# Linear attention and a residual MLP on one core: a rewrite with two woven TensorE streams

## The chip, the cores and the metric

The kernel runs on one core of a Trainium2 chip. A core has five engines that run side by side and are ordered by semaphores: TensorE (PE), VectorE (DVE), ScalarE (ACT), GpSimd (POOL) and SyncE (SP), which issues most DMAs. The metric is the time of one execution on the device, in microseconds, as the median of several runs. Lower is better.

## The reference

There are 8 batches, 8 heads, 576 tokens and 64 channels a head (512 channels in all). All inputs and the output are float32.

```python
kv  = einsum('bhsd,bhse->bhde', k, v)          # 64 x 64 a head
att = einsum('bhsd,bhde->bhse', q, kv)
att = att / sqrt(mean(att*att, -1) + 1e-6) * g_norm
x   = att as [batch, token, 512]
a1  = alpha1 * x + beta1
u   = x + lam * einsum('ts,bsd->btd', w_tok, a1)    # w_tok 576 x 576
a2  = alpha2 * u + beta2
out = u + lam * (relu(a2 @ w_ch1) @ w_ch2)          # 512 -> 2048 -> 512
```

## The kernel before, in words

A batch's 576 tokens are 4 chunks of 128 (tokens p*4 + c, so that one partition loads 4 adjacent tokens) and a tail of 64. Weights and the moving side of the MLP are bf16; the attention runs in f32r, a rounded float32 with 4 bytes.

The steps of a batch, with their lines in the profile:

- Loads on SP's queue: `load_main` (L324) and `load_tail` (L330) bring k, v and q as float32 into `kf`, `vf`, `qf` and the tails.
- Rounding on DVE: `round_kv` (L347, L351) and `permute_q` (L355) copy them to f32r and put the 4 chunks outermost.
- `kv_groups` (L366, L369): for each pair of heads five matmuls with 128 tokens (the last 64) in the contraction; the moving side is 256 columns, four heads of v. Only the two diagonal 64 x 64 blocks of the result are used. DVE (L389) copies each times g_norm into `kvc`, and ACT (L392) copies it once more without g, so that `kvc` gives both the scaled and the plain result.
- `qt_groups` (L407, exits L414 and L420): 20 PE transposes of q.
- `qkv_groups` (L451): for each of 5 chunks four matmuls of 256 columns, one a pair of heads: 128 columns with g and 128 without. ACT squares the plain half (L459), DVE sums (L461), ACT takes the root (L464), DVE inverts (L467), multiplies (L471, this is x), forms `rt` = x * alpha1 * lam (L476) and adds beta1's share (L480).
- `tok_groups` (L496): for each of 5 chunks five matmuls of 512 columns with the transposed w_tok; the odd tail chunk computes 128 rows of which 64 are used. DVE adds (L502). POOL forms a2 = u * alpha2 + beta2 in two passes (L506, L509).
- `ut_groups` (L527, exit ACT L533): PE transposes of a2 in bf16, the tails of two batches together.
- `ch1_groups`: an even batch has 16 x 4 matmuls of 512 columns (L560), an odd one 16 x 8 of 320 columns (L575), which take in the tails of both batches. ACT applies relu into `ht` (L551).
- `ch2_groups` (L597): 16 matmuls of 512 columns for each of 4 chunks (5 in odd batches). DVE adds u (L606); SP stores (L609, L613). lam is in `w2` already: it was multiplied in when w_ch2 was loaded (DVE and POOL, L746); w_ch1 is cast by ACT (L736).

The order of the work is a planner's. Every operation is recorded with an engine, a cost in us, what it reads and writes, and a priority (its place in the program). `schedule` plays the engines forward with these costs: each takes the first operation in its queue that is ready, PE from the first 8, the others from the first 400, and PSUM banks are given out in pairs or singly. The resulting order on each engine is then fixed and only semaphores act on the chip. A PE operation is a whole group (4 to 16 matmuls), so groups of different steps alternate but matmuls within a group are together:

```python
for b in range(NB):
    ch1, ch2 = list(ch1_groups(b)), list(ch2_groups(b))
    ...
    merge(ch1, list(qkv_groups(b + 1)), 0, len(ch1) * 5 // 8)
    ...
    for f in tok_groups(b + 1):
        f()
    merge(ch2[:8], [], 0, 0)
    ...
    merge(ch2[8:], fill, 0, len(ch2) - 10)   # fill: ut(b+1), kv(b+2), qt(b+2)
```

At the start q, k, v of batch 0, w_tok and six vectors (each broadcast to 128 partitions by its DMA) are loaded first, then the weights. w_tok is transposed by PE in float32 (L674, exits ACT L679) and its row sums are formed by DVE (`wsums`, L691).

Of the kernel before, what the change touches and what calls it, by code (L numbers as in the profile page):

```python
# [13 lines left out]
NB = 8  # L14
# [5 lines left out]
TP = 640  # L20


class Op:
    __slots__ = ("eng", "cost", "fn", "deps", "raw", "alloc", "tiles", "pri", "idx",
                 "start", "end", "pos", "waits", "inc", "lat", "clock", "sem")

    def __init__(self, eng, cost, fn, pri, idx):
        self.eng, self.cost, self.fn, self.pri, self.idx = eng, cost, fn, pri, idx
        self.deps, self.raw = set(), set()
        self.alloc, self.tiles = [], []  # L30
        self.start = self.end = self.pos = None
        self.waits, self.inc, self.lat, self.clock, self.sem = [], False, 0.0, None, None


class PTile:


    def __init__(self, prog, n):
        self.prog, self.n, self.bank, self.ops, self.prev = prog, n, None, [], set()

    def ap(self, parts=slice(0, 128)):
        return self.prog.ps[parts, self.bank:self.bank + self.n, :]

    def flat(self, parts=slice(0, 128)):
        return self.ap(parts).rearrange("p b f -> p (b f)")


class Prog:

    COMPUTE = ("PE", "ACT", "DVE", "POOL")

    def __init__(self, nc, stack):
        self.nc, self.stack = nc, stack
        self.ops, self.lastw, self.readers = [], {}, {}
        self.ps = stack.enter_context(nc.psum_tensor("ps", [128, 8, 512], F32))
        self.eng = {"PE": nc.tensor, "ACT": nc.scalar, "DVE": nc.vector,
                    "POOL": nc.gpsimd, "SP": nc.sync, "AQ": nc.scalar}
        self.bias = 0  # L60
        self.pe_window = 8

    def ptile(self, n):
        return PTile(self, n)

    def op(self, eng, cost, fn, r=(), w=(), pri=0.0, dma_us=None):
        o = Op(eng, cost, fn, len(self.ops) + pri + self.bias, len(self.ops))
        o.lat = dma_us
        self.ops.append(o)
        for key in r:  # L70
            if isinstance(key, PTile):

                o.deps.update(y for y in key.ops if y.eng != eng)
                key.ops.append(o)
                o.tiles.append(key)
# [4 lines left out]
        for key in w:  # L80
            if isinstance(key, PTile):
                if not key.ops:
                    o.alloc.append(key)
                key.ops.append(o)
                o.tiles.append(key)
# [8 lines left out]
            self.readers[key] = []  # L94
        return o

    def schedule(self):
        queues = {}
        for o in self.ops:
            queues.setdefault(o.eng, []).append(o)  # L100
        for e, q in queues.items():
            q.sort(key=lambda o: o.pri)
        free = {e: 0.0 for e in queues}
        order = {e: [] for e in queues}
        left = len(self.ops)
        owner = [None] * 8
        dma_free = 0.0
        t = 0.0
        events = set()

        def done(o, t):
            return o.end is not None and o.end <= t + 1e-9

        def bank_ok(b, t):
            tile = owner[b]
            return tile is None or all(done(x, t) for x in tile.ops)

        def bank_since(b):
            tile = owner[b]
            return -1.0 if tile is None else max(x.end for x in tile.ops)  # L120

        def place(tile, t):
            if tile.n == 2:
                c = [b for b in (0, 2, 4, 6) if bank_ok(b, t) and bank_ok(b + 1, t)]
                if not c:
                    return None
                return min(c, key=lambda b: max(bank_since(b), bank_since(b + 1)))
            c = [b for b in range(8) if bank_ok(b, t)]
            if not c:
                return None  # L130
            return min(c, key=lambda b: (bank_ok(b ^ 1, t), bank_since(b)))

        while left:
            progressed = False
            for e, q in queues.items():
                while q and free[e] <= t + 1e-9:
                    pick = None
                    cands = q[:self.pe_window] if e == "PE" else q[:400]
                    for o in cands:
                        if not all(done(y, t) for y in o.deps):  # L140
                            continue
                        if any(place(tile, t) is None for tile in o.alloc):
                            continue
                        pick = o
                        break
                    if pick is None:
                        break
                    q.remove(pick)
                    for tile in pick.alloc:
                        tile.bank = place(tile, t)  # L150
                        for b in range(tile.bank, tile.bank + tile.n):
                            if owner[b] is not None:
                                pick.deps.update(owner[b].ops)
                            owner[b] = tile
                    pick.start = t
                    free[e] = t + pick.cost
                    if pick.lat is not None:
                        dma_free = max(dma_free, t) + pick.lat
                        pick.end = dma_free + 2.0
                    else:  # L160
                        pick.end = t + pick.cost + 0.15
                    pick.pos = len(order[e])
                    order[e].append(pick)
                    events.add(pick.end)
                    events.add(free[e])
                    left -= 1
                    progressed = True
            if left:
                nxt = [x for x in events if x > t + 1e-9]
                if not nxt:  # L170
                    raise RuntimeError("stuck at %r" % t)
                t = min(nxt)
                events = set(nxt)
        self.order = order
        self.sequence = sorted(self.ops, key=lambda o: (o.start, o.idx))

    def queue_of(self, e):
        return "ACT" if e == "AQ" else e

    def synchronize(self):  # L180

        known = {}
        pos = {}
        for o in self.sequence:
            e = self.queue_of(o.eng)
            o.pos = pos.get(e, 0)
            pos[e] = o.pos + 1
            k = known.setdefault(e, {})
            need = {}
            for y in o.deps:  # L190
                ye = self.queue_of(y.eng)
                if y.lat is not None:
                    key, v = ("dma", y.idx), 1
                else:
                    key, v = ye, y.pos + 1
                    if ye == e and e != "POOL" and y not in o.raw:
                        continue
                    if ye == e and e == "PE":
                        continue
# [10 lines left out]
            o.clock = dict(k)  # L210
            if o.lat is not None:
                o.clock[("dma", o.idx)] = 1
                o.inc = True
            else:
                o.clock[e] = o.pos + 1

    def emit(self):
        nc = self.nc
        sems = {e: self.stack.enter_context(nc.semaphore("s_" + e)) for e in self.COMPUTE}
        count = {e: 0 for e in self.COMPUTE}  # L220
        val = {}
        for o in self.sequence:
            if o.lat is not None:
                val[o.idx] = (self.stack.enter_context(nc.semaphore("d%d" % o.idx)), 16)
            elif o.inc:
                count[o.eng] += 1
                val[o.idx] = (sems[o.eng], count[o.eng])
        block = self.stack.enter_context(nc.Block("main"))

        @block.gpsimd  # L230
        def _(gps):
            for o in self.sequence:
                eng = self.eng[o.eng]
                for y in o.waits:
                    eng.wait_ge(*val[y.idx])
                ins = o.fn(eng)
                if o.lat is not None:
                    ins.then_inc(val[o.idx][0], 16)
                elif o.inc:
                    ins.then_inc(sems[o.eng], 1)  # L240
            for o in self.sequence:
                if o.lat is not None:
# [3 lines left out]
def bass_transnormer_attn__then__resmlp_affine_kernel(  # L246
# [15 lines left out]
    with ExitStack() as stack:  # L262
# [5 lines left out]
        ident = sb("ident", [128, 128], F32)  # L268
        identb = sb("identb", [128, 128], BF16)
        e1_bc = sb("e1_bc", [128, DM], F32)  # L270
# [5 lines left out]
        eps = sb("eps", [128, 1], F32)  # L276
        wsum = sb("wsum", [128, 6], F32)
        wsp = sb("wsp", [128, 4], F32)
        kf = sb("kf", [128, NH, 4, DH], F32)
        vf = sb("vf", [128, NH, 4, DH], F32)  # L280
        qf = sb("qf", [128, NH, 4, DH], F32)
# [545 lines left out]
```

## Time and profile before

| | |
|---|---|
| runs | 421.88, 422.67, 422.98 us; median 422.67 |
| span of the profiled execution | 422.0 us, 5398 instructions; the profile gives no time of this execution beside its span |
| median of the runs less the span | 0.65 us |
| busy, share of the span | PE 376.5 us (89%), DVE 226.8 (54%), ACT 167.5 (40%), POOL 120.3 (29%) |
| weight loads on PE (PEld) | 227.8 us (54%) |
| DMA | 49.15 MB, 116 GB/s over the span |
| granted PE clock | 0.964 of full, mean |

How to read it: an engine's busy time is an average over stages. PE is pipelined: the recorded time of a matmul (379 ns for L597) overlaps the next one's, so what a matmul costs is the distance between starts in a run of equal ones. PEld lies beside PE. The chain of waits goes back from the last instruction and names at each step what released it.

### The profile page before, as it was taken

The numbers are of one execution on the slowest core, as the hardware profiler recorded it, in microseconds if no ns is written. First come the engines' busy times: TensorE is split into PE (matmuls) and PEld (weight loads), VectorE is DVE, ScalarE is ACT, GpSimd is POOL, SyncE is SP. The second block draws the span as 40 slices with busy tenths as digits, with TensorE's granted clock in tenths as the row PEclk, the third lists the DMA queues.
The fourth block names the chain that finished last, engine by engine and source line by source line (L and its number), as shares of the span: only waits on it lengthen the run. The fifth ranks groups of instructions, "written<-read, shape, count | busy, mean of one in ns | idle before, by whom it ended". The sixth has DMA issues, their size and how long they took to land.

```text
span 422.0 us, 5398 instructions
## 1 busy us (share of the span) xinstructions
PE 376.5 (89%) x2193; PEld 227.8 (54%) x2193; DVE 226.8 (54%) x371; ACT 167.5 (40%) x263; POOL 120.3 (29%) x92
## 2 busy tenths in 40 slices
PE   0574755899899999999999999999999999999994
PEld 0563242444677465545775565446774665446642
DVE  3439894995587336862786165743783228620011
ACT  1069142540477025712673135503770157215600
POOL 1000499309300830038003800074007400290000
PEclk9985695999999999999999999999999999999999
DMA  8999999202293019501670139001100201011012
GB/s 241 331 349 302 359 265 351 84 0 99 71 282 85 2 75 263 125 1 61 214 163 2 50 124 284 6 26 51 37 2 0 76 25 25 2 50 51 2 50 75
DMA packets 49128, 49.15 MB, mean 116 GB/s; under 512 B 14608, under 2 KB 39184, under 8 KB 49104
## 3 DMA queue, kind: packets, MB, share of 16 engines
q1 hardware_dynamic: 46672, 46.29, 37.7%
q10 hardware_dynamic: 2432, 2.52, 1.9%
q8 instruction: 17, 0.28, 0.3%
q14 instruction: 7, 0.06, 0.0%
HBM read 39.37 MB, written 9.44 MB: 116 GB/s over the span
## 4 chain that ended last, share of the span: by engine, by line
PE 69%; POOL 12%; DVE 7%; DMA 4%; ACT 3%; issue 2%; POOLq 0%; SPq 0%
PE ps L597 22%; PE ps L575 17%; PE ps L560 12%; POOL a1f L506 6%; POOL a2b L509 6%; PE ps L496 6%; PE ps L451 4%; PE ps L407 4%; DMA qf<-in_q_dram 4%; PE ps L366 2%; PE ps L527 1%; DVE xm L480 1%; DVE xm L502 1%; DVE krt L351 1%; PE ps L674 1%
## 5 line engine op out<-in xcount | busy, mean ns | idle before, releaser
L597 PE MATMUL ps<-w,ht 128*128 128x512 bf16 x576 | 135.3, 379 | 0.0
L506 POOL TENSOR_TENSOR a1f<-xm,a_bc 128x512 f32<-128x512 f32 x32 | 42.8, 1337 | 255.3 <-DVE xm L502 253.5
L551 ACT ACTIVATE ht<-ps 128x640 bf16<-128x640 f32 (+1 forms) x96 | 77.8, 810 | 50.2 <-PE ps L560 25.3
L597 PEld LDWEIGHTS ps<-w,ht 128*128 128x128 bf16 x576 | 54.1, 98 | 57.0 <-DVE xm L502 0.6
L575 PE MATMUL ps<-a2t,w 128*128 128x320 bf16 x512 | 73.0, 299 | 0.0
L606 DVE TENSOR_TENSOR xm<-ps,xm 128x512 f32<-128x512 f32 x32 | 22.1, 690 | 83.1 <-PE ps L597 83.0
L533 ACT ACTIVATE a2t<-ps 128x1024 bf16<-128x1024 bf16 (+1 forms) x20 | 18.8, 938 | 116.8 <-PE ps L527 116.8
L560 PE MATMUL ps<-a2t,w 128*128 128x512 bf16 x256 | 61.2, 388 | 2.6 <-ACT a2t L533 1.1
L575 PEld LDWEIGHTS ps<-a2t,w 128*128 128x128 bf16 x512 | 48.7, 98 | 19.9 <-ACT a2t L533 0.3
L509 POOL TENSOR_TENSOR a2b<-a1f,b_bc 128x512 bf16<-128x512 f32 (+1 forms) x40 | 54.2, 1355 | 3.1
L496 PE MATMUL ps<-rt,wt 128*128 128x512 bf16 x200 | 46.9, 393 | 7.5 <-DVE rt L476 7.5
L560 PEld LDWEIGHTS ps<-a2t,w 128*128 128x128 bf16 x256 | 23.8, 100 | 30.4 <-issue 1.8
L366 PE MATMUL ps<-vr,kr 128*128 128x256 f32 x128 | 26.5, 332 | 13.8 <-DVE vrt L351 13.8
L496 PEld LDWEIGHTS ps<-rt,wt 128*128 128x128 bf16 x200 | 20.0, 100 | 32.5 <-DVE rt L476 7.8
L451 PE MATMUL ps<-kvc,qt 128*128 128x256 f32 x160 | 33.2, 338 | 2.7 <-ACT kvc L392 2.7
L461 DVE TENSOR_REDUCE small<-sq 128x8 f32<-128x512 f32 (+1 forms) x40 | 27.1, 677 | 11.4 <-ACT sq L459 11.3
L502 DVE TENSOR_TENSOR xm<-ps,xm 128x512 f32<-128x512 f32 x32 | 22.0, 690 | 16.9 <-PE ps L496 16.7
L366 PEld LDWEIGHTS ps<-vr,kr 128*128 128x128 f32 x128 | 20.3, 206 | 16.9 <-DVE vrt L351 14.3
L451 PEld LDWEIGHTS ps<-kvc,qt 128*128 128x128 f32 x160 | 25.7, 210 | 6.8 <-ACT kvc L392 3.0
L414 ACT ACTIVATE qt<-ps 128x1024 fp32r<-128x1024 f32 x16 | 16.4, 1024 | 22.3 <-PE ps L407 22.3
L480 DVE SCALAR_TENSOR_TENSOR xm<-e_bc,wsum,xm 128x512 f32<-128x512 f32 x32 | 25.0, 782 | 0.2
L459 ACT ACTIVATE sq<-ps 128x512 f32<-128x512 f32 (+1 forms) x40 | 23.6, 591 | 2.9 <-PE ps L451 2.8
(57 smaller groups left out, 294.6 us busy)
## 6 DMA issues: line engine op xcount, KB each, us to landing
kf<-in_k_dram SPq DMA_DIRECT2D x8, 1024.0 KB, 7.4
qf<-in_q_dram SPq DMA_DIRECT2D x8, 1024.0 KB, 9.6
stg<-in_moe_w_ch_dram SPq DMA_DIRECT2D x8, 1024.0 KB, 10.8
out_dram<-xm SPq DMA_DIRECT2D x32, 256.0 KB, 2.3
vf<-in_v_dram SPq DMA_DIRECT2D x7, 1024.0 KB, 9.0
vf<-in_v_dram ACTq DMA_DIRECT2D x1, 1024.0 KB, 9.8
kft<-in_k_dram SPq DMA_DIRECT2D x8, 128.0 KB, 9.3
qft<-in_q_dram SPq DMA_DIRECT2D x8, 128.0 KB, 9.0
```

The lines of the kernel that those rows point to most:

```text
L366: e.matmul(o, flat(kr[:, c, 2 * pr:2 * pr + 2, :]), flat(vr[:, c, u0:u0 + 4, :]), start=(c == 0), stop=False)
L451: m = e.matmul(t.flat()[:, 256 * pr:256 * pr + 256], qt[:, pr, 128 * c:128 * c + 128], kvc[:, pr, :], start=True, stop=True)
L461: P.op("DVE", dve_us(512), lambda e: e.tensor_reduce(out=small[rows, sms], in_=sq[rows, sqs], axis=AX.X, op=ALU.add), r=[("sq", sqs)], w=[ ...
L480: P.op("DVE", dve_us(560), lambda e: e.scalar_tensor_tensor(out=x, in0=e2_bc[rows, :], scalar=wsum[rows, wc:wc + 1], in1=x, op0=ALU.mult, ...
L496: m = e.matmul(t.flat(), wt[:, ws, col:col + 128], rt[:, sc, :], start=(sc == 0), stop=(sc == 4))
L502: P.op("DVE", dve_us(512), lambda e: e.tensor_tensor(out=x, in0=t.flat(rows), in1=x, op=ALU.add), r=[t, xkey(b, c)], w=[xkey(b, c)], pri=-100)
L506: P.op("POOL", pool_us(512), lambda e: e.tensor_tensor(out=a1f[rows, af, :], in0=x, in1=a2_bc[rows, :], op=ALU.mult), r=[xkey(b, c), "a2"] ...
L509: P.op("POOL", pool_us(512), lambda e: e.tensor_tensor(out=a2b[rows, c, :], in0=a1f[rows, af, :], in1=b2_bc[rows, :], op=ALU.add), r=[("a1 ...
L551: P.op("ACT", act_us(n), lambda e: e.activation(dst, src(), ACT.Relu), r=[t], w=key)
L560: m = e.matmul(t.ap()[:, i, :], w1[:, dj, 128 * (fj + i):128 * (fj + i) + 128], a2t[:, dj, 0:512], start=(dj == 0), stop=(dj == 3))
L575: m = e.matmul(t.ap()[:, i, 0:320], w1[:, dj, 128 * fj:128 * fj + 128], a2t[:, dj, 320 * i:320 * i + 320], start=(dj == 0), stop=(dj == 3))
L597: m = e.matmul(t.flat(), ht[:, fj, 128 * c:128 * c + 128], w2[:, fj, :], start=(fj == 0), stop=(fj == 15))
```

## The change

The planner and the body are written anew. What it does:

1. **Two PE streams.** ch1 and ch2 form the stream `main` (PSUM banks 0 to 3), everything else `fill` (banks 4 to 7). `schedule` takes main operations strictly in order and a ready fill operation beside each. A fill operation marked slow (128-column f32) is woven with one main operation: their matmuls alternate one by one. The order on every engine is fixed by the planner as before.
2. **Attention per head over two token chunks.** q, k, v keep the layout of the load. A stationary operand is one head's two adjacent chunks (128 columns: 2 tokens x 64). kv of a head is two matmuls of 128 columns whose two diagonal blocks are added (ACT copies one, DVE adds the other, ACT copies the sum to the lower half), with two more for the tails of 4 heads. q is transposed by matmuls with an f32r identity. att comes from 128-column matmuls, 4 heads to a bank; x and `rm` are formed from it for 2 chunks at once, and g_norm is applied later by POOL (and is folded into alpha1's row for `rm`).
3. **Casting loads.** q from batch 1 on, k and v from batch 2 on, w_tok, w_ch1 and w_ch2 are loaded by DMAs issued on POOL's queue that change the type on the way. DVE's rounding is left for batches 0 and 1 only.
4. **a2 by transposing DMA from the third batch on** (index 2): POOL forms a2 as before, SP issues `dma_start_transpose`. For batches 0 and 1 PE transposes xm and the exit applies alpha2 and beta2.
5. **lam at the PSUM exit.** w2 holds w_ch2 itself; DVE multiplies the exit of ch2 by lam into one of three `tmp` buffers, POOL adds it to u (DVE in the last batch).
6. The tails of two batches are done in one set of tok matmuls with 64-row outputs side by side, ch1 always has 512 columns, with a tail of 128 columns in odd batches. x has four buffers, a2 transposed three. The six vectors are loaded as single rows and broadcast by PE; w_tok's row sums come from one-column matmuls.

The core of the diff, new side (lines as in the new file):

```diff
+    # schedule(), PE's turn
+    m = main[0] if main and can(main[0], t) else None
+    f = None
+    if not (last_fill and m):
+        for o in fill[:10]:
+            if can(o, t, o.margin if m else 0.0):
+                f = o
+                break
+    ...
+    if f is not None and m is not None and f.kind == "w":
+        ...
+        self.sequence.append((f, m))        # woven one by one
```

```diff
-            for src, dst, n in ((kf, kr, "k"), (vf, vr, "v")):
-                P.op("DVE", dve_us(2048, 2), lambda e, s=src, d=dst: e.tensor_copy(
+    def load_kv(b):                                           # L584, L586; q: fill_q L576, L579
+        for n, x, m, tl in (("k", k, kr, krt), ("v", v, vr, vrt)):
+            P.dma("POOL", n + "r", 1 << 20, lambda e, x=x, m=m: e.dma_start(
+                md(m[:]), src_main(x, b, 0, 8)), w=[(n, 0), (n, 1)], issue=1.2)
+            P.dma("POOL", n + "rt", 1 << 17, ...)
+    def load_w1(i):                                           # L520; load_w2 L526; w_tok L512, L515
+        wdma[i] = P.dma("POOL", "w1_%d" % i, 1 << 20, lambda e: e.dma_start(w1[...], moe_w_ch1[...]), ...)
```

```diff
-                        e.matmul(o, flat(kr[:, c, 2 * pr:2 * pr + 2, :]),
-                                 flat(vr[:, c, u0:u0 + 4, :]), ...)                  # 256 columns
+                fns += [lambda e, h=h, o=o, c=c: e.matmul(                         # kv(), L616
+                    t.ap()[:, o], fl(kr[:, h, c:c + 2, :]), fl(vr[:, h, c:c + 2, :]), ...) for c in (0, 2)]
+                    fns.append(lambda e, h=h, c=c, o=o: e.matmul(                  # qtr(), L668; tail L650
+                        t.ap()[:, o], fl(qr[:, h, c:c + 2, :]), identr[:], start=True, stop=True))
+                fns = [lambda e, h=h: e.matmul(                                    # norm(), L701; tail L727
+                    t.ap()[:, 128 * (h % 4):128 * (h % 4) + 128], qt[:, h, cp, :],
+                    kvc[:, i, h, :], start=True, stop=True) for h in range(4 * hh, 4 * hh + 4)]
```

```diff
+        def a2_dma(b, c):                                     # from b = 2; a2_pe L838, L847 before
+            P.op("POOL", ..., a1f[:, s] = x * a2_bc)          # L878
+            P.op("POOL", ..., a2b[:, c] = a1f[:, s] + b2_bc)  # L881
+            P.dma("SP", "t%d" % c, 1 << 18, lambda e: e.dma_start_transpose(dst, a2b[:, c]), ...)  # L885
-                P.op("DVE", dve_us(512), lambda e: e.tensor_tensor(out=x, in0=t.flat(), in1=x, op=ALU.add), ...)
+            P.op("DVE", ..., tmp[:, s] = t.ap() * lam_bc)     # finish(), L944
+            P.op("DVE" if last else "POOL", ..., x = x + tmp[:, s])   # L949
```

Other new lines: ch1 is L900 with its tail L913, ch2 L928, relu L895, tok L800 with the tails L818, bias1 L786, the multiplication by g_norm L778.

## The prediction

> **What bounds the kernel now.** I read the table by stage first: the stages cut at the starts of the channel step (ch1) of each batch.
>
> ```profile
> core 0: us, PE busy (x) PEld busy (x) DVE busy (x) ACT busy (x) POOL busy (x), PEclk, DMA share, GB/s
> ...
> 20.00:45.00 25.00, 13.82 (x65) 11.49 (x63) 17.80 (x39) 16.78 (x26) 0.00 (x0) 0.69 1.09 325
> ...
> 60.00:72.00 12.00, 3.71 (x15) 1.81 (x16) 7.28 (x8) 3.02 (x6) 11.92 (x6) 0.65 1.03 328
> ...
> 163.20:206.46 43.26, 42.55 (x240) 23.83 (x238) 24.66 (x43) 18.18 (x28) 12.69 (x10) 1.00 0.36 99
> 206.46:253.60 47.14, 47.14 (x307) 30.58 (x305) 26.86 (x45) 20.48 (x36) 12.66 (x10) 1.00 0.40 111
> ```
>
> There are two regimes. From 116 us to the end PE is busy in all but 0.7 us of each pair of stages, at full clock; an even and an odd batch together take 43.26 + 47.14 = 90.4 us, and no other engine reaches 60%. Up to 72 us the DMA engines are full (325 GB/s) and PE is half idle at a low clock. The chain of waits in order of time shows how that start ends, and gives clean rates for long runs of one matmul:
>
> ```profile
> 59.40 2.23 POOL a1f L506
> ...
> 64.87 2.25 POOL a2b L509
> 67.17 1.05 PE ps L527 x8
> 68.24 1.03 ACT a2t L533
> 69.32 3.61 PE ps L560 x8
> ...
> 135.94 5.40 PE ps L496 x25
> ...
> 157.60 0.87 PE ps L407 x8
> ...
> 383.10 16.30 PE ps L575 x120
> 399.39 17.28 PE ps L597 x80
> 416.70 0.69 DVE xtl L606
> ```
>
> The first ch1 matmul starts at 69.3 us, behind POOL's two passes for a2, transposes and an eviction. A 512-column bf16 matmul costs 0.216 us (5.40/25, 17.28/80), a 320-column one 0.136, a 128-column f32 transpose 0.109 (0.87/8). After the last matmul 422.0 - 416.7 = 5.3 us remain. The timeline of PE prices the rest:
>
> ```profile
> 119.58 0.74 PE L451 MATMUL ps<-kvc,qt 128*128 128x256 f32 x4
> 120.17 3.43 PE L575 MATMUL ps<-a2t,w 128*128 128x320 bf16 x24
> 123.33 0.75 PE L451 MATMUL ps<-kvc,qt 128*128 128x256 f32 x4
> 123.92 2.35 PE L575 MATMUL ps<-a2t,w 128*128 128x320 bf16 x16
> ```
>
> From 120.17 to 123.92 are 3.75 us; 24 x 0.136 = 3.27 of them are L575, so four 256-column f32r matmuls cost 0.48, or 0.120 each. L366 with L369, taken the same way, costs 0.118 each. Eight 128-column bf16 transposes (L527) between two L597 runs cost 0.056 each.
>
> **Attention at N=128 and weaving.** Before, a pair of batches has main work (ch1 and ch2) of 64 x 0.217 + 128 x 0.136 + 144 x 0.216 = 62.4 us, and 28.0 us of the rest: 50 tok matmuls 10.8, 40 kv 4.7, 40 qkv 4.8, 40 q transposes 4.4, 36 a2 transposes 2.0, idle and switching 1.3. After, main is 256 + 16 matmuls of 512 columns and 64 of 128: 272 x 0.216 + 64 x 0.056 = 62.3, the same. The attention keeps its counts (40 kv, 40 norm, 32 q transposes and 8 of half width) but all have 128 columns, and the new scheduler sets each between two 512-column matmuls of the main stream. No row shows a 128-column f32 matmul there. Bounds: 0.056 (L527, the time for 128 columns to pass) and 0.109 (L407, back to back; a weight load, 0.15 mean in that group, is then in the way). I take 0.060, near the low end, since 0.216 us of another matmul now lies over each weight load. tok falls from 25 to 20 matmuls a batch, with the tail rows of two batches done together in ten 64-row matmuls, two side by side (0.108 each if they overlap, 0.216 if not; I take 0.108). The pair becomes 62.3 + 112 x 0.060 + 8 x 0.03 + 40 x 0.216 + 10 x 0.108 = 79.0 us: 11.4 less.
>
> **All of PE after the first ch1.** By the order in which the new kernel issues: 1088 x 0.216 = 235.0 and 256 x 0.056 = 14.3 for ch1 and ch2; tok 140 x 0.216 + 40 x 0.108 = 34.5; 410 woven 128-column matmuls (kv, norm, q, and the PE transposes of a2 for batches 0 and 1) x 0.060 = 24.6; 28 of 64 columns 0.8. Sum 309.2 us.
>
> **The start.** Casting loads remove the rounding copies on DVE (L347, L351, L355: 41 us in all) and the weight casts (ACT L736 7.6, POOL and DVE L746 16). Batch 0's a2 comes from PE transposes of xm with alpha2 and beta2 applied at the PSUM exit, so POOL's 59.4 to 67.2 falls away. What sets the start now is w_tok's main part: POOL issues it last, behind four quarters of w1, and it waits there for half of k. Ahead of it or with it come q, k, v (3.54 MB on SP), w1 4.19, w_tok 1.33: 9.06 MB at 0.325 MB/us = 28, plus 2.2 to the first byte and some 2 to land: 32. If SP's k and v of batch 1 (2.36 MB) share the engines, 39. I take 35. Before, these transposes begin at 28.3, so this step alone is a loss of 7. After it: 25 transposes with five ACT exits of 0.64, 4 us; 30 one-column matmuls for wsum, at 0.056 to 0.109, 2.5; eight bias and eight tok adds of 256 columns on DVE, 0.51 and 0.42 (L480 0.78 and L502 0.69 less 256/960), 7.5; 18 transposes and kv matmuls at a low clock and one exit, 3.5. First ch1 at 35 + 4 + 2.5 + 7.5 + 3.5 = 52.5 (44 to 60), against 69.3.
>
> **What lies beside PE.** a2 from batch 2 costs POOL two passes a chunk as before, then a transposing DMA on SP. No row has one: between the 2.3 and 4.1 us that SP's stores take to land, or up to the 16.3 of a load in the crowded start; I take 3, a store's, as the steady part is not crowded. SP serves its queue in order, so stores wait behind a transpose that waits for POOL, and the other way round. Counted from the first ch1 on PE, tok of batch 2 yields its four chunks from 64 to 70 us and its ch1 starts at 83; in between POOL has 8 a2 passes and 3 additions, 11 x 1.27 = 14, so 64 + 0.7 + 14 + 3 = 82, just in time. Later batches have over 25 us there. lam at the exit: DVE's multiply (L944) takes the place of L606, 0.69 each, and POOL gets 31 additions of 1.27. Three tmp buffers lie between: if POOL is late, DVE's multiply waits, then the four PSUM banks of the main stream, then PE. Per pair DVE has 44 us and ACT 38 of 79; both stay covered.
>
> POOL is the tight one. While the attention runs ahead (the first 211 us after the first ch1) it has 108 passes x 1.27 = 137 us and 38 DMA issues. For an issue no POOL row exists; SP's take 0.37 to 0.61 when nothing is queued before them and 3.60, 5.05, 5.88 in the crowded start. I take 1.2 (the small end, as steady DMA share is under 0.5): 137 + 46 = 183 of 211. That fits, but the loads of batch 4 stand in POOL's queue behind a2 and the additions and are needed at 82 us after the first ch1, about when they land. I put 3 us of stall there (0 to 15).
>
> [...]
>
> **The sum.** 52.5 + 309.2 + 5.3 + 3 = 370; the span of before is 422.0 and the median of its runs 0.65 more, so 370.7, say 371. About 0.3% (1.3 us) can be told from no change.
>
> **Rivals.** (1) *Weave without gain*: each of the 410 costs 0.109: +20, and 390. For it: PEld of f32 takes 0.2 a load against 0.1 for bf16. Against: with 256 columns 0.120 was reached, so most of a load hides behind only 0.107 of streaming. (2) *Casting loads at half rate* (0.16 MB/us): w_tok lands some 6 us later; a batch of q, k, v takes 21 us instead of 10, so batch 3 (freed at 42, needed at 58) costs 8 and batch 4 about 5 more: 390. Nothing in the trace casts in a DMA. (3) *Slower: POOL becomes the bound.* With x us an issue, its stretch lasts 137 + 38x, and after it come some 98 us of main work without attention: 52.5 + 137 + 38x + 98 + 6 = 293.5 + 38x. Over x = 1.95 it is the bound; over x = 3.4 the kernel is slower than before; at the 3.60 of SP's queue in the start it takes 430. For it: POOL was only 29% busy and now carries a third queue's work, in order. Against: the steady DMA engines are mostly idle. (4) *Nothing changes*, a coincidence of these, 422.
>
> **Chances.** The sum, 0.55; weave without gain, 0.13; late loads or a part of the POOL wait, 0.14; POOL the bound and slower, 0.16; same, 0.02. Faster 0.82, same 0.02, slower 0.16. Range: the start at 44 and no stall give 359, a start earlier still 352; the top takes in rivals 1 and 2 and half of both together, 410. That leaves out the slower case and a little below.
>
> **What would show it.** Right: first ch1 near 52 us; in the steady part 128-column f32 matmuls alternating with 512-column ones, each two in about 0.276 us; PE busy without gaps; POOL 80 to 90% busy up to about 260 us. Wrong: gaps on PE before L616 (kv) or L900 (ch1) released by a DMA, POOL issues over 2 us, or two woven matmuls in 0.325 us or more.

## The result and the profile after

| | before | after |
|---|---|---|
| median of the runs | 422.27 us (420.95 to 422.98) | 393.52 us (391.74 to 395.88) |
| span of the profiled execution | 422.0 us | 391.9 us |
| first ch1 matmul | 69.3 us | 57.9 us |
| from there to the end of the last matmul | 347.4 us | 329.4 us |
| after the last matmul | 5.3 us | 4.6 us |

The ratio is 0.932, with a 95% interval of 0.927 to 0.936: faster by 6.8%. The forecast was 371 us with a range of 352 to 410. The direction and the range hold; the point is some 22 us too low, and most of what follows is about those 22 us. (The profiled execution of e7_kv_split below took 406.2 us, 1.7% above the fastest of its kernel, so only its rows are used.)

The table by stage of the kernel after, with the columns of the one shown of before:

```profile
core 0: us, PE busy (x) PEld busy (x) DVE busy (x) ACT busy (x) POOL busy (x), PEclk, DMA share, GB/s
27.40:42.40 15.00, 13.80 (x42) 9.79 (x42) 8.55 (x18) 4.85 (x13) 2.52 (x2) 1.00 0.93 241
...
118.00:142.00 24.00, 24.00 (x186) 16.92 (x183) 15.13 (x26) 9.42 (x21) 19.69 (x17) 1.00 0.72 136
160.00:184.00 24.00, 22.91 (x141) 13.94 (x138) 15.70 (x30) 10.68 (x23) 20.99 (x18) 1.00 1.03 183
...
243.00:247.00 4.00, 1.68 (x11) 0.93 (x8) 0.69 (x1) 0.60 (x1) 3.13 (x3) 1.00 1.61 335
247.00:251.00 4.00, 4.00 (x22) 3.65 (x22) 0.42 (x1) 0.98 (x2) 3.03 (x3) 0.62 1.22 266
```

PE is full from the first ch1 on, apart from a few holes, and POOL is 82 to 87% busy beside it in these two stretches (19.69 and 20.99 of 24 us). From the first ch1 to 260 us it is 67% busy (134.5 of 202.1 us), less than the 80 to 90% forecast. New to the eye are the last two rows: a hole on PE, and behind it a stretch with a clock of 0.62 though PE has work all the time. The start, by the chain of waits in order of time:

```profile
7.38 16.71 DMA xm<-in_v_dram
...
27.43 1.97 PE ps L616 x8
...
29.82 5.41 PE ps L555 x6
...
39.00 3.51 PE ps L564 x16
...
49.24 6.53 PE ps L800 x40
```

w_tok is not in it. It landed at 29.3 us (issued at 18.57, 10.7 us on the way), and the first transpose of it stands at 42.44 on PE's timeline: PE was working in order through kv, three broadcasts (L555), norm and one-column matmuls (L564).

The price of a 128-column f32 matmul in the weave is read from starts to starts in the timeline of PE:

```profile
95.05 0.38 PE L928 MATMUL ps<-w,ht 128*128 128x512 bf16 x1
95.26 0.27 PE L838 MATMUL ps<-ident,xm 128*128 128x128 f32 x1
95.37 0.38 PE L928 MATMUL ps<-w,ht 128*128 128x512 bf16 x1
...
100.05 0.41 PE L616 MATMUL ps<-vr,kr 128*128 128x128 f32 x1
...
102.02 0.27 PE L616 MATMUL ps<-vr,kr 128*128 128x128 f32 x1
...
109.73 0.41 PE L701 MATMUL ps<-kvc,qt 128*128 128x128 f32 x1
109.98 0.39 PE L900 MATMUL ps<-a2m,w 128*128 128x512 bf16 x1
110.02 0.41 PE L701 MATMUL ps<-kvc,qt 128*128 128x128 f32 x1
```

There are three prices, not one. An L701 and an L900 in turn take 0.292 us (five pairs from 109.73 to 111.19), so 0.076 for the L701. A unit of ten kv matmuls among four L900 takes 102.02 - 100.05 = 1.97 us, so (1.97 - 4 x 0.216)/10 = 0.110: two or three kv matmuls stand in a row there. A transpose (L838) with an L928 takes 0.325, so 0.109. The last two are about what such matmuls cost without any weave (0.109 for the transposes of the kernel before, 0.108 for kv in the run e1_unwoven below).

The holes on PE, in the list of waits (us in total, times, longest):

```profile
PE ps L616 <- DMA vrt<-in_v_dram: 3.4, 2, 2.3
...
PE ps L668 <- DVE kvc L632: 1.3, 1, 1.3
...
PE ps L800 <- DVE rtl L770: 0.5, 1, 0.5
```

These are 5.2 us after the first ch1. The clock costs 1.7 more: I cut the stretch after the first ch1 into windows of 3 us and summed (1 - clock) x length. What is left, 334.0 - 5.2 - 1.7 = 327.1 us, is PE's own work with the end. That split is made for every run below.

### The profile page after: what moved, and what is told of

It is laid out like the page before. It is cut to its first block, busy times and chain, and to the rows that moved or that the text cites. A ratio compares the mean times of both kernels' runs of the same rounds, so it can differ in the third digit from the quotient of the medians.

```text
span 391.9 us, 5426 instructions
## 1 busy us (share of the span) xinstructions
PE 365.0 (93%) x2163; PEld 219.4 (56%) x2163; DVE 195.2 (50%) x329; ACT 163.0 (42%) x323; POOL 198.6 (51%) x180
## 4 chain that ended last, share of the span: by engine, by line
PE 72%; DVE 11%; DMA 8%; POOL 3%; issue 2%; ACT 2%; SPq 2%
PE ps L928 25%; PE ps L900 24%; PE ps L800 8%; DMA xm<-in_v_dram 4%; DMA vrt<-in_v_dram 4%; PE ps L913 3%; PE ps L616 3%; DVE rm L770 3%; PE ps L701 2%; PE ps L668 2%; POOL a1f L878 2%; PE ps L555 1%; DVE xm L766 1%; DVE small L758 1%; DVE rtl L770 1%
## 5 line engine op out<-in xcount | busy, mean ns | idle before, releaser
L900 PE MATMUL ps<-a2m,w 128*128 128x512 bf16 x512 | 132.3, 386 | 0.0
L928 PE MATMUL ps<-w,ht 128*128 128x512 bf16 x512 | 127.5, 382 | 0.0
L895 ACT ACTIVATE ht<-ps 128x512 bf16<-128x512 f32 x128 | 76.2, 598 | 84.3 <-PE ps L900 83.0
L928 PEld LDWEIGHTS ps<-w,ht 128*128 128x128 bf16 x512 | 49.3, 98 | 51.7 <-issue 0.4
L900 PEld LDWEIGHTS ps<-a2m,w 128*128 128x128 bf16 x512 | 49.2, 98 | 48.8 <-issue 0.8
L944 DVE TENSOR_TENSOR tmp<-ps,lam_bc 128x512 f32<-128x512 f32 x36 | 24.8, 688 | 97.9 <-PE ps L928 97.8
L949 POOL TENSOR_TENSOR xm<-xm,tmp 128x512 f32<-128x512 f32 x28 | 37.1, 1326 | 57.5 <-DVE tmp L944 57.4
L778 POOL TENSOR_TENSOR xm<-xm,g_bc 128x512 f32<-128x512 f32 x32 | 43.6, 1374 | 31.9 <-DVE rm L770 31.8
L701 PE MATMUL ps<-kvc,qt 128*128 128x128 f32 x128 | 37.6, 412 | 1.2 <-ACT lam_bc L558 1.2
L616 PE MATMUL ps<-vr,kr 128*128 128x128 f32 x128 | 27.5, 349 | 10.5 <-ACT vrt L602 3.8
L800 PE MATMUL ps<-rm,wt 128*128 128x512 bf16 (+1 forms) x144 | 35.2, 372 | 0.7 <-DVE rtl L770 0.5
L881 POOL TENSOR_TENSOR a2b<-a1f,b_bc 128x512 bf16<-128x512 f32 x27 | 34.1, 1271 | 0.3
L786 DVE SCALAR_TENSOR_TENSOR xm<-e_bc,wsum,xm 128x512 f32<-128x512 f32 (+1 forms) x36 | 32.4, 942 | 1.6 <-POOL xm L778 1.4
L668 PE MATMUL ps<-identr,qr 128*128 128x128 f32 x112 | 32.0, 395 | 1.3 <-DVE kvc L632 1.3
L616 PEld LDWEIGHTS ps<-vr,kr 128*128 128x128 f32 x128 | 24.2, 220 | 13.6 <-DMA vrt<-in_v_dram 4.4
L755 ACT ACTIVATE sq<-ps 128x512 f32<-128x512 f32 (+2 forms) x41 | 23.5, 582 | 14.5 <-PE ps L701 9.4
L673 ACT ACTIVATE qt<-ps 128x512 fp32r<-128x512 f32 x32 | 19.2, 600 | 24.6 <-PE ps L668 19.0
L701 PEld LDWEIGHTS ps<-kvc,qt 128*128 128x128 f32 x128 | 26.2, 217 | 4.5 <-ACT kvc L635 1.5
L770 DVE TENSOR_TENSOR rm<-xm,e_bc 128x512 bf16<-128x512 f32 x32 | 27.2, 862 | 0.1
L807 DVE TENSOR_TENSOR xm<-ps,xm 128x512 f32<-128x512 f32 (+1 forms) x36 | 21.5, 624 | 10.8 <-PE ps L800 10.6
```

What stands on the lines that cost most here:

```text
L616: fns += [lambda e, h=h, o=o, c=c: e.matmul(t.ap()[:, o], fl(kr[:, h, c:c + 2, :]), fl(vr[:, h, c:c + 2, :]), start=(h % 4 == 0 and c == 0 ...
L668: fns.append(lambda e, h=h, c=c, o=o: e.matmul(t.ap()[:, o], fl(qr[:, h, c:c + 2, :]), identr[:], start=True, stop=True))
L701: fns = [lambda e, h=h: e.matmul(t.ap()[:, 128 * (h % 4):128 * (h % 4) + 128], qt[:, h, cp, :], kvc[:, i, h, :], start=True, stop=True) fo ...
L770: P.op("DVE", dve(n), lambda e: e.tensor_tensor(out=r, in0=x, in1=bc(e1_bc[rs, fs]), op=ALU.mult), r=xks + ["e1"], w=rks)
L778: P.op("POOL", pool(n), lambda e: e.tensor_tensor(out=hv(gx), in0=hv(gx), in1=gv, op=ALU.mult), r=xks + ["g"], w=xks)
L800: lambda e, sc=sc: e.matmul(t.ap()[:, cs], wt[:, sc if sc < 4 else tail_w(b), 128 * c:128 * c + 128], (rm[:, b % 2, sc, cs] if sc < 4 else ...
```

## The experiments

All ratios are to the kernel before, run on the same chip; the kernel after has 0.932 (0.927 to 0.936). "Rest" is the profiled span less the first ch1.

| run | median us | ratio (95%) | first ch1 | rest | gaps | clock | rest less both |
|---|---|---|---|---|---|---|---|
| after | 393.5 | 0.932 | 57.9 | 334.0 | 5.2 | 1.7 | 327.1 |
| e1_unwoven | 401.5 | 0.948 (0.946 to 0.951) | 61.9 | 338.1 | 2.5 | 0 | 335.6 |
| e2_bf16 | 386.5 | 0.913 (0.911 to 0.916) | 58.4 | 326.6 | 7.9 | 3.4 | 315.3 |
| e3_a2_pe | 400.4 | 0.946 (0.943 to 0.949) | 60.9 | 338.0 | 0.3 | 0 | 337.7 |
| e4_start | 388.9 | 0.919 (0.913 to 0.926) | 55.8 | 332.4 | 5.6 | 0 | 326.8 |
| e5_no_lam | 387.9 | 0.916 (0.914 to 0.919) | 59.7 | 326.6 | 1.3 | 0 | 325.3 |
| e7_kv_split | 402.4 | 0.950 (0.946 to 0.954) | 60.6 | 343.7 | 12.4 | 6.8 | 324.5 |
| e8_start_split | 398.7 | 0.943 (0.940 to 0.945) | 52.3 | 343.5 | 12.1 | 6.8 | 324.6 |
| e9_start_split_bf16 | 383.3 | 0.906 (0.904 to 0.908) | 52.2 | 329.3 | 11.3 | 1.7 | 316.3 |
| e10_loads_first | 395.3 | 0.934 (0.931 to 0.937) | 56.4 | 337.1 | 6.9 | 3.4 | 326.8 |
| e11_start_split_loads | 397.1 | 0.938 (0.935 to 0.941) | 53.8 | 340.1 | 9.6 | 6.8 | 323.7 |
| e12_dve_all | 402.2 | 0.950 (0.947 to 0.953) | 52.8 | 347.9 | 15.4 | 8.5 | 324.0 |
| e13_all_bf16 | 393.2 | 0.928 (0.925 to 0.931) | 53.0 | 338.1 | 18.7 | 5.1 | 314.3 |

Where a stretch at a low clock begins inside a gap, both columns count it, so that the last one is too low by 0.2 us in e2_bf16, 0.4 in e7, 0.7 in e8, 1.6 in e11, 1.1 in e12 and 1.9 in e13.

Two things are seen at once. The last column follows PE's prices in every run, to within some 2 us. And the median often does not follow the last column, because gaps and the clock take up to 23 us. The first ch1 moves by up to 5.5 us between runs with the same start, as the second half of v lands earlier or later (kv of that half starts at 26.3 us in e10_loads_first and at 30.7 in e1_unwoven, and the first ch1 follows 30 to 31 us behind in both), so a start is judged from there.

**What the weave brings.**

```diff
     # Prog.woven
-    if i < n and (j >= k or i * k <= j * n):
+    if i < n:
```

> The two units that PE takes together keep their places, but the matmuls of the fill unit are issued first and then those of the main unit, no longer one by one. Same instructions, same planner's order of units. Theory A (the weave hides part of a 128-column f32 matmul's weight load: 0.077 to 0.092 us woven in the trace, 0.109 in a run of equal ones): some 410 matmuls x 0.019 to 0.032 = 8 to 13 us slower, 402 to 406. Rival B (the weave brings nothing on the chip): 393.5. By the 0.060 of the prediction the loss would be 410 x 0.049 = 20 us, 413.

Measured: 0.948 against 0.932, some 7 us slower; 335.6 against 327.1 us of PE work, so the weave is worth 8.5 us and fewer gaps gave one part back. Its timeline:

```profile
108.55 0.75 PE L668 MATMUL ps<-identr,qr 128*128 128x128 f32 x4
109.14 1.04 PE L900 MATMUL ps<-a2m,w 128*128 128x512 bf16 x4
109.83 0.75 PE L668 MATMUL ps<-identr,qr 128*128 128x128 f32 x4
```

Four and four take 1.28 us, so 0.104 for an L668, against 0.076 woven. Kv's unit costs 1.94 us, as much as woven. Theory A holds for the 252 matmuls of norm and of q's transposes (252 x 0.028 = 7.1 us), and not for kv.

**What remains of the price.**

```diff
-        kr = sb("kr", [128, NH, 4, DH], F32R)
+        kr = sb("kr", [128, NH, 4, DH], BF16)
         # the same for vr, qr, krt, vrt, qrt, qt, qtt, kvc, identr
```

> k, v, q, their transposes, kv and the identity of q's transposes are bf16 instead of f32r (the loads cast to bf16); the precision of the attention is lower. Same matmul counts, same planner's order. Theory A (the 0.02 to 0.03 us a woven matmul above the 0.056 of 128 streamed columns is the load of 4-byte weights, 0.22 us in the weight-load rows against 0.098 for bf16): 360 matmuls x 0.03 = 11 us less, 382 or a little under, with PE's stalls left as they are. Rival B (it is the short matmul among long ones that costs, whatever its type): 393. Rival C (the casting loads' written bytes matter: they halve, so the gaps before L616 of 3.4 us go as well): 379.

```profile
103.05 0.22 PE L668 MATMUL ps<-identr,qr 128*128 128x128 bf16 x1
103.10 0.38 PE L900 MATMUL ps<-a2m,w 128*128 128x512 bf16 x1
103.32 0.22 PE L668 MATMUL ps<-identr,qr 128*128 128x128 bf16 x1
```

A pair takes 0.27 us, 0.055 for the bf16 matmul, and the kv unit 1.42 us, 0.056 each. PE's work falls by 11.8 us, what theory A said; gaps and clock take 4.4 of it back, and the median falls by 7.7 (0.0182 x 422). So the extra of 0.02 to 0.055 us is a matter of the 4-byte operands. That it is their weight load (0.22 us in the rows, 0.098 for bf16) fits, but a width that slows something else would look the same. Rival C falls: the loads write half the bytes and the gaps before L616 are still 2.1 us, on two places.

**Is POOL, with the loads in its queue, the bound?**

```diff
-                if b > 1:
-                    a2_dma(b, c)
-            if b < 2:
-                a2_pe(b)
+            a2_pe(b)
```

> a2 comes from PE transposes with alpha2 and beta2 at the exit in all batches, as the new kernel does it in batches 0 and 1; 54 POOL passes (69 us) and 27 transposing DMAs go, 108 f32 transposes come onto PE, 27 exits onto ACT and DVE. Theory A (after the first ch1 PE is the bound and POOL, 51% busy, is covered): 108 x 0.077 to 0.109 = 8 to 12 us slower, less at most the 3.4 us of gaps that PE has before L616: 398 to 405. Rival B (POOL's queue holds the loads back and costs more than the trace shows on PE): 390 or less.

Measured: 0.946. PE's work grows by 10.6 us (108 x 0.109 = 11.8), the gaps shrink from 5.2 to 0.3 and the clock loss goes. Theory A. So a2 on POOL with the transposing DMAs is worth 4 us by the profiles' rest and 6 by the medians, and POOL is not the bound; its load costs at most the 6.6 us by which gaps and clock fell.

**What sets the first ch1.**

```diff
-        broadcast(1, lam_bc, "lam")
-        broadcast(3, a2_bc, "a2")
-        broadcast(4, b2_bc, "b2")
+            P.dma("SP", "bc_" + key, 1 << 18, lambda e, x=x, d=d: e.dma_start(
+                d[:], x.partition_broadcast(128)), w=[key])
```

> lam, alpha2 and beta2 are broadcast to 128 partitions by three DMAs on SP's queue, behind the k and v of batch 1, instead of by three one-row f32 matmuls pairs on PE (L555, 5.4 us between 29.8 and 35.2 us) and three ACT exits. Theory A (what sets the first ch1 is PE's own chain, in order: broadcasts, norm, one-column matmuls, transposes of w_tok, which had landed 13 us before PE came to it): first ch1 from 57.9 to 53, in all 5 us less, 388.5. Rival B (PE waited there for DVE's norm anyway and the broadcasts filled the wait): first ch1 at 57 to 58, 393.

Measured: 0.919, some 5 us less. In its timeline kv of the second half of batch 0 stands at 30.30 and the first ch1 at 55.80, 25.5 us later; in the kernel after the two are 27.43 and 57.92, 30.5 apart. The 5.0 us between are the 5.4 of L555. Theory A: PE's own order is the start's chain.

**kv in smaller units.**

```diff
-            P.mm("fill", 128, fns, r=[("k", hh), ...], w=[t], slow=True)
+            for i0, i1 in ((0, 4), (4, 8), (8, 10)):
+                P.mm("fill", 128, fns[i0:i1], r=[("k", hh), ...], w=[t], slow=True)
```

> The ten matmuls of four heads' kv, one unit for the planner until now, become three units of 4, 4 and 2, so that each is woven with a main unit of four matmuls of its own and no two or three kv matmuls stand in a row. Same instructions. Theory A (the weave pays only one to one: in the trace of the new kernel L668 and L900 in turn cost 0.292 us a pair, so 0.076 for L668, while ten L616 among four L900 took 1.97 us, so 0.110 each, no less than the 0.108 of the unwoven kernel): 140 x 0.034 = 4.8 us less, 388.7. Rival B (kv costs 0.110 for its own reasons, four matmuls adding into one bank): 393.5.

Neither forecast: 0.950, some 8 us slower. Yet the matmuls did as theory A said: L616 and L902 (the line of ch1 in this kernel) in turn take 0.292 us, and PE's work is down by 2.2 us (4.8 expected; the 0.4 us counted twice is put back). What it lost is waits:

```profile
PE ps L616 <- DMA vrt<-in_v_dram: 7.7, 3, 3.8
...
PE ps L670 <- DMA qr<-in_q_dram: 2.6, 1, 2.6
```

**The same with the start's edit.** This is e4_start's and e7_kv_split's edits together.

> The broadcasts of lam, alpha2 and beta2 by DMA and kv in units of 4, 4 and 2, together; same precision as the new kernel. If both gains hold and add: 393.5 - 4.7 - 4.8 = 384. If kv's split brings nothing: 389.

Measured: 0.943; the start gains, the split loses, as each did alone. Its largest gap shows how. POOL's queue first, then PE:

```profile
243.67 1.29 POOL L883 TENSOR_TENSOR a2b<-a1f,b_bc 128x512 bf16<-128x512 f32 x1
244.88 0.94 POOL L584 DMA_DIRECT2D kr<-in_k_dram  x1
245.81 0.70 POOL L586 DMA_DIRECT2D krt<-in_k_dram  x1
246.51 1.30 POOL L951 TENSOR_TENSOR xt<-xt,tmp 128x512 f32<-128x512 f32 x1
247.73 0.92 POOL L584 DMA_DIRECT2D vr<-in_v_dram  x1
248.64 0.69 POOL L586 DMA_DIRECT2D vrt<-in_v_dram  x1
```

```profile
259.65 0.47 PE L616 MATMUL ps<-vr,kr 128*128 128x128 f32 x1 [3.76 <-DMA vrt<-in_v_dram]
259.93 0.65 PE L902 MATMUL ps<-a2m,w 128*128 128x512 bf16 x1
...
260.49 0.65 PE L902 MATMUL ps<-a2m,w 128*128 128x512 bf16 x1
```

From kr's issue to vrt's landing are 259.65 - 244.88 = 14.8 us for 2.36 MB. The planner's code prices loads at 360 GB/s, 6.6 us for these, with 1.3 us ahead and 1.0 behind: 8.9 us if they are issued together. A PE order fixed by that price has nothing else in it when the load is late. Behind the gap a pair of matmuls takes 0.56 us instead of 0.292 until about 265. The windows say it of the clock:

```profile
259.60:262.60 3.00, 2.94 (x10) 0.50 1.17 130
262.60:265.60 3.00, 3.00 (x10) 0.59 0.02 2
265.60:268.60 3.00, 3.00 (x16) 1.00 0.01 3
```

The gap of 3.76 us cost another 3 x 0.50 + 3 x 0.41 = 2.7 us.

**Both, in bf16.** e2_bf16's edit on top.

> The same two edits and the attention's operands in bf16. Theory A (a woven 128-column matmul then costs 0.055, as in the trace with bf16, where L668 and L900 in turn took 0.2705 us a pair): start as before less 4.7; bf16 less 7 to 8; the split should bring only a little more, as a bf16 matmul costs 0.055 in a row as well: 393.5 - 4.7 - 7.5 = 381, 379 to 382. Rival B (bf16 kv gains by the split as f32r does): 377.

Measured: 0.906 (0.904 to 0.908), 383.3 us: the fastest of all, 2.7% under the kernel after, in lower precision. By ratio it is 382.6 us against the 422.27 of the first runs, near the 379 to 382 of theory A, but the parts differ: PE's work falls as expected, and the gaps grow from 5.2 to 11.3 us. The split adds nothing here over the other two edits: PE's work is 316.3, and 315.3 without it.

**lam left out.**

```diff
-                out=tmp[:, s], in0=t.ap(), in1=lam_bc[:], op=ALU.mult), ...
-                 lambda e: e.tensor_tensor(out=x, in0=x, in1=tmp[:, s], op=ALU.add), ...
+                out=x, in0=t.ap(), in1=x, op=ALU.add), r=ks + [t], w=ks, pri=-1000)
```

> lam is left out: DVE adds u to the exit of ch2 in one pass and POOL's 32 additions go (the output lacks the factor lam). Theory A (lam's share of the work is covered on DVE and POOL): within 1 us of the new kernel, 393, the end the same or 0.7 us shorter. Rival B (POOL's additions, 37 us in all, stand ahead of the casting loads in its queue and cause the 3.4 us of gaps before L616): 390.

Measured: 0.916, some 6.5 us less, and rival B's side: no gap before L616 is left on a load, the clock stays at 1.00, and 1.8 us of the rest are gone as well. My forecast that the additions are covered was wrong for this kernel. But the planner's order changes with the edit as well, and no run separates the two.

**The loads ahead in POOL's queue.**

```diff
-                    md(m[:]), src_main(x, b, 0, 8)), w=[(n, 0), (n, 1)], issue=1.2)
+                    md(m[:]), src_main(x, b, 0, 8)), w=[(n, 0), (n, 1)], issue=1.2,
+                    pri=-1000)          # the same for the tails and for q
```

> The loads of k, v and q on POOL's queue get the planner's first priority, so that fewer passes for a2 stand between them; nothing else. In the new kernel the four loads that end with vrt were issued over 16.5 us (158.1 to 174.7), with five a2 passes between, and landed after the kv matmuls wanted them. Theory A (the loads' place in POOL's queue makes the gaps before L616, 3.4 us, and the drop of the granted clock after the longer one, 0.58 over 4 us, so 1.7 us): 3.4 + 1.7 = 5 us less, 388.5. Rival B (the loads are late because they move only some 200 GB/s at a full DMA share, whatever their place): 393.

Measured: 0.934, no gain. Theory A's cause was removed, and its gain did not come: no gap before kv (L617 here) waits for a load any more, and others stand in their place:

```profile
PE ps L617 <- DVE xm L767: 3.0, 2, 2.0
PE ps L669 <- DVE kvc L633: 2.1, 1, 2.1
...
PE ps L819 <- DVE xm L808: 1.8, 1, 1.8
```

They sum to 6.9 us, with 3.4 of clock. The result is near rival B's 393, but not for its reason: the loads came in time. Now kv waits for a PSUM bank that DVE's norm has still to read (L767). Why DVE is late there stands in the timelines of POOL, DVE and PE before the longer of the two gaps:

```profile
205.05 2.50 POOL L882 TENSOR_TENSOR a2b<-a1f,b_bc 128x512 bf16<-128x512 f32 x2
205.38 3.94 DVE L771 TENSOR_TENSOR rm<-xm,e_bc 128x512 bf16<-128x512 f32 x1
207.51 1.26 POOL L879 TENSOR_TENSOR a1f<-xm,a_bc 128x512 f32<-128x512 f32 x1
209.25 0.68 DVE L767 TENSOR_TENSOR xm<-ps,small 128x512 f32<-128x512 f32 x1
209.98 0.33 PE L617 MATMUL ps<-vr,kr 128*128 128x128 f32 x1 [2.02 <-DVE xm L767]
```

L771, a pass of 0.68 us where POOL is idle, took 3.94 and ended 0.55 us after the last of three POOL passes for a2 without a pause. Before the other gap, of 1.0 us, it took 3.12. Both excesses are longer than the gaps behind them, so these gaps come from POOL through DVE and not from the loads. The 1.3 us before L668 in the kernel after has the same look: two such passes (L770) took 3.92 us ahead of it.

**Everything together.** e8_start_split with the loads first; then also the additions of u on DVE; then bf16.

```diff
-            P.op("DVE" if last else "POOL", dve(512) if last else pool(512),
+            P.op("DVE", dve(512),
```

> The start's broadcasts by DMA, kv in units of 4, 4 and 2, and the loads first. Theory A (the split was worth its 4.8 us on PE, but PE then outran the loads: gaps of 12 us instead of 5 and a lower clock after each): with the loads first it comes to 393.5 - 5 - 4.8 - 5 = 379; with half of the gaps left 385. Rival B (the split costs by itself, the loads have no part in it): as the same two edits without it, 397.

> As the last, and the additions of u after ch2 go from POOL to DVE in all batches (32 x 1.33 us off POOL, 32 x 0.69 onto DVE). Theory A (POOL's queue is what delays the loads): 1 to 5 us less than without it, 376 to 382. Rival B (DVE, 50% busy, delays norm's chain by as much): the same as without it or slower.

> As the last, with the attention's operands in bf16. Theory A (a woven 128-column matmul costs 0.055 instead of 0.076): 390 x 0.021 = 8 us less than with f32r, 370 to 374. Rival B (faster PE only lengthens the gaps before the loads land): 378 or more.

Measured: 0.938, 0.950 and 0.928. Theory A's forecasts of 379, 376 to 382 and 370 to 374 all failed, and the numbers of the rivals hold: 397.1 for 397, slower still with DVE's additions, and 393 for 378 or more. But the first rival's reason, that the loads have no part in it, does not: e11_start_split_loads still waits for vrt for 5.0 us in one gap. PE's work is no less than with the two edits alone (with the part counted twice put back, 325.3 and 325.1 against 325.3 in f32r, 316.2 against 316.3 in bf16), and gaps and clock come to 15, 23 and 22 us. Taking 41 us off POOL (busy 204.6 to 163.3) and putting 15 on DVE (198.6 to 213.7) made things worse: e12_dve_all waits for vrt for 8.4 us. The moved additions read two SBUF tensors like L771, and they stretch like it: 0.64 to 0.69 us where POOL is idle (21 of them), 1.47 in the median and up to 3.18 beside a POOL pass (11). So this run does not say what POOL's relief alone is worth. What all these runs have in common is that the order on PE is fixed ahead by prices; every edit shuffles it, and where kv or norm is placed a few us before its operand is there on the chip, a gap opens. Two prices are off by the traces: the loads (14.8 against 8.9 us) and DVE's passes beside POOL. How much of the gaps each is worth no run has isolated; one with other prices in the planner would.

## Why the prediction was right, and where it was off

By its own terms, against the profiled 391.9 us:

| step | predicted | measured | off |
|---|---|---|---|
| first ch1 | 52.5 | 57.9 | +5.4 |
| PE's work after it | 309.2 | 329.4 - 5.2 - 1.7 = 322.5 | +13.3 |
| stalls | 3 | 5.2 of gaps + 1.7 of clock | +3.9 |
| end | 5.3 | 4.6 | -0.7 |
| sum | 370 | 391.9 | +21.9 |

Three of the four terms were too small, so hardly any error cancelled; the range held because its top had room for rivals 1 and 2.

- **The woven matmul, 410 x 0.060 = 24.6.** This is the term that was mis-sized. By the three prices read above it is 130 kv x 0.110 + 252 x 0.076 + 28 transposes x 0.109 = 36.5, 12 us more. With the other terms measured (256 L913 x 0.0573, 40 tail rows of tok x 0.120 instead of 0.108, 28 of 64 columns at 0.046) the sum is 322.5, as measured. The step that failed was to take one price for all and to put it near the low bound, because 512 columns would lie over every weight load. A saving shows only where the turns are one to one, and even there 0.02 us over 0.055 remain. I also wrote that kv, norm and q would each stand between two 512-column matmuls; a unit of ten kv matmuls meets a main unit of four. "Weave without gain" was half true: it holds for kv and the transposes, and not for the 252. That its 390 is nearer to the result than the sum is luck, since its 20 us for the weave are 8 too many and the start and the stalls, which it left alone, made up for them.
- **The start.** Its end was off by 5.4 us: the transposes of w_tok began at 42.4 instead of 35, and the steps from there on took 15.5 us instead of 17.5. The 0.27 us that it took off DVE's passes for 256 columns less is near the traces: L691 of before takes 0.669 us with 512 columns and 0.408 with 256, and the halved passes of the kernel after took 0.48 (L786) and 0.42 (L807), for 0.51 and 0.42. The landing of w_tok did not set it: it landed at 29.3, before the 35 taken, and was used 13 us later. The chain is v's second half (landed at 24.1) and then PE in order. What the prediction left out of the start are the f32 matmuls with one row, 5.4 us for three broadcasts (L555) and 3.5 for the columns (L564); e4_start shows that the first come straight off. Nearly all of the start ran at half the clock (to 53.4 us, see the last section), which the prediction assumed only for its last 3.5 us.
- **Stalls.** Right in kind: L616 waiting for loads in POOL's queue, 3.4 us, but for later batches, at 180 and 246 us. What was missing are 1.8 us of waits for DVE, 1.3 of them behind passes that POOL had stretched, and that a gap can lower the clock behind it (to 0.50 for 3.4 us behind the one of 2.32 us).
- **POOL.** An issue of k, v or q behind the first ch1 takes 0.69 to 0.95 us, not 1.2, and the transposing DMA 2.5 us to land, for the 3 taken (5.8 for the tails). In the 211 us behind the first ch1 POOL has 89 passes and 36 issues, 143 us, where the prediction had 108, 38 and 183. POOL as the bound needed 1.95 us an issue, a slower kernel 3.4; e3_a2_pe confirms that it is far from it. One issue was longer, in the start, beside a copy of DVE:

```profile
47.94 1.55 POOL L526 DMA_DIRECT2D w<-in_moe_w_ch_dram  x1
47.98 1.21 DVE L599 CAST kr<-xm 128x2048 fp32r<-128x2048 f32 x1
```

  The issue took 1.55 us where the three others of its line took 0.80 to 0.82, and ended 0.3 us after the copy; five more runs, in which the same two meet, have it too (1.55 or 1.56). That the copy held the issue back fits; no run separates it. Behind the first ch1 the casting loads have left DVE no such copy, and no issue took more than 0.95 us.
- **SP's queue.** That it is served in order fits the trace of before: DVE ended an exit (L606) at 207.95 us, and its store is issued at 211.73, behind the loads of v and q (from 207.18 and 209.75 us, the last to 211.69). A store that waits behind a transposing DMA does not show after: 36 of the 40 stores are issued 0.03 to 0.05 us behind their addition (L949), and the other four, the second ones of the tails, 0.55 to 0.63 us behind it.
- **Casting loads at half rate.** Not met. Where a batch's k, v and q are issued together, from 61.99 and from 104.33 us, the 3.54 MB took 15.1 and 16.0 us (0.23 and 0.22 MB/us), between the 10 and the 21 of the prediction. From 231.44 us on k and v alone took 14.8 us, 0.159 MB/us, as in e8_start_split; but here the issues are spread over 7 us and there over 4.5, and in both q's load, stores and transposing DMAs run beside them. The cost of 20 us did not come: later batches have tens of us for it, and only where kv stands close does it show.
- **Main work, tok, the end.** As predicted: L800 0.216, L913 0.0573; from the tail of ch1 in batch 5 (303.98) to that in batch 7 (366.26), where no attention is left, are 62.28 us for the 62.3 of a pair.
- **The signs named beforehand.** Two woven matmuls take 0.292 us, between the 0.276 named for right and the 0.325 for wrong, and with a transpose 0.325; POOL is as busy as named only from 118 to 184 us; the gaps before L616 are one of the signs for wrong, and small.

## What to carry to other kernels

Price a short matmul by its neighbours: read start-to-start distances for one to one, for two or three in a row, and for transposes: here the weave paid only one to one, and not at all for transposes. Where an order is fixed ahead by prices, less work on the busiest engine is not less time until the prices of the loads, and of DVE's passes beside POOL, are right: eight of the twelve edits here took 1.8 us or more off PE's own work, and three of those eight (e7, e8, e12) made the kernel clearly slower, by gaps and clock alone. Split a span into work, gaps and clock loss before you judge an edit by its total.

## What the runs showed of the hardware

The clock behind a gap. The kernel after and e4_start have the same gap before kv (2.32 and 2.39 us); by windows of 1 us of the first of them

```profile
247.00:248.00 1.00, 1.00 (x9) 0.99 1.47 390
248.00:249.00 1.00, 1.00 (x6) 0.50 1.87 340
249.00:250.00 1.00, 1.00 (x6) 0.50 1.42 290
250.00:251.00 1.00, 1.00 (x6) 0.50 0.12 43
251.00:252.00 1.00, 1.00 (x6) 0.80 0.00 0
252.00:253.00 1.00, 1.00 (x8) 1.00 0.00 0
```

the clock goes to one half 1.8 us after PE has resumed, for 3.4 us; in e4_start it stays at 1.00. The losses over all runs are 0, 1.7, 3.4, 5.1, 6.8 and 8.5 us, whole multiples of 1.7: half of 3.4 us each. A gap of 1.80 us in e7_kv_split has such a stretch behind it, and one of 2.75 us in e9_start_split_bf16 has none. What fits is where the gap falls: in each run the changes of the clock lie whole multiples of 3.41 us apart (in the kernel after at 53.42, 247.98 and 251.39). Cut into stretches on this grid, the 13 profiles have 17 at full clock in which PE was idle for 1.94 us or more, and each is followed by one at half clock; none with 1.65 us or less is; of the four between, those with 1.68 and 1.80 are and those with 1.77 and 1.90 are not. In the kernel after 1.68 us of the gap lay in one stretch; in e4_start the gap was split into 1.39 and 1.00.

DVE beside POOL. In the kernel after, a pass of DVE that reads two SBUF tensors can take longer beside a pass of POOL: L786 with 512 columns 0.69 to 0.74 us where POOL is idle (16 of them) and up to 1.87 beside it (12, median 1.75), L770 0.64 to 0.69 (18) and up to 3.27 (23, of which 12 took 0.72 or less). The passes that read PSUM (L766, L807, L944) stay at 0.70 or less beside POOL.

A woven f32r matmul of 128 columns costs 0.076 us one to one with a 512-column bf16 one, and a bf16 one 0.055. At the start the clock column of the kernel after says 1.00 while its matmuls run at half speed: a 256-column L800 takes 0.213 us up to 53.4 us and 0.107 after. Its trace has no clock record ahead of 53.4 us, and e4_start, which has one, gives 0.50 for 14.5 to 52 us. There the distances between starts are to be believed, not the column.
